# Swapping the first two gate products of an attention-plus-gMLP kernel on one Trainium2 core

## The chip, the cores and the metric

One Trainium2 chip, one core. The metric is the device time of one execution in microseconds (us), the median of several. "Span" is the time from the first to the last instruction of the one execution that a profile shows; it is some 1.7 to 1.8 us shorter than that execution's device time. Ratios are computed as the mean time of one kernel's runs over that of the other's of the same rounds, so they are not quite the ratio of the medians that are quoted beside them.

## The reference, cut to what matters

```python
xn = _layernorm(x)                        # 2048 tokens x 512
return x + A(xn, wqkv, wo) + B(xn, w_in, w_sp, b_sp, w_out)
# A: attention with 32 heads of 16, window of 8 keys two tokens apart
# B: z = gelu(xn @ w_in); z1 = first half (688); z2 = layernorm(second half)
#    g = w_sp @ z2 + b_sp; (z1 * g) @ w_out
```

Everything that follows happens in the first 27 of 201 us, where the normalised tokens are turned (transposed) so that TensorE can multiply them, and the first products for B (called z2 in the kernel) and A (q and k) are made.

## The kernel before

The 16 tiles of 128 tokens stand in four blocks: tile `4*tb + j` belongs to block `j`. The tokens `z2.0` and `z1.3` of the order string mean `z2_mm(2, 0)` and `z2_mm(1, 3)`, so the first tile of block 2 and the last of block 1; `zg` is the GELU that empties the product, `q2.2` a k product of block 2, `qc` the cast that empties it.

```python
ps_mm = ctx.enter_context(tc.tile_pool(name="ps_mm", bufs=3, space=PSUM))   # three PSUM buffers rotate
...
def tr_dma(i):                            # turn one tile by a DMA, issued from SyncE
    SP.dma_start_transpose(xnT[:, :, i * P:(i + 1) * P], xall[:, j, tb, :])

def zmm(i, wz):                           # 8 matmuls of 344 columns, L257
    pz = ps_mm.tile([P, 2, TBS], F32, name="pz", tag="mm")
    for hh in range(2):
        for kc in range(C):
            PE.matmul(pz[:, hh, 0:FHALF], xnT[:, kc, i * P:(i + 1) * P], wz[...], ...)

def z2_gelu(j, tb):                       # L275, empties pz
    A.activation(z2[:, i, :]..., tiles.pop(("z", j, tb))..., ACT.Gelu_apprx_tanh, accum_out=...)
...
    load_x(SP, 3, 0, 4)                   # x of block 3: four plain loads
    ...
    for i in i2:                          # block 2: normalise, then turn
        ln_apply(i)
        tr_dma(i)
    ...
    qk_part(pqs[0], 1, 3, 2, 4)           # last q/k product of block 1
    ln_root(blk_cols(3))                  # ScalarE: root of the variances of block 3
    qk_copy(pqs[0], 1, 3, 2, 4)           # ScalarE: cast that empties pqs[0]
    for i in i3:
        ln_apply(i)
        tr_dma(i)
    ...                                   # and then the steps of ORDER, one after the other
```

In these traces each engine's instructions stand in the order in which the program names them, so a product that waits holds up those named after it: in the kernel before z2.0 waited 0.60 us for its tile, and z1.3, whose tile had long landed, came behind it. The waits are on semaphores, which the trace records.

## Time and profile before

| | kernel before |
|---|---|
| time, median of the first three runs | 202.72 us (202.51 to 202.82) |
| time, median of all six runs of the comparison | 202.45 us (202.07 to 202.82) |
| span of the profiled execution | 200.8 us |
| TensorE (PE) busy | 196.3 us, 98% |
| VectorE (DVE) busy | 184.8 us, 92% |
| ScalarE (ACT) busy | 104.1 us, 52% |

TensorE works nearly without a break, so a change can win time in two ways: take work from TensorE, or fill one of its gaps. Its list of waits, its timeline and the chain tell which gaps there are; those lines stand in the prediction below. A busy share of 98% alone would not tell, because it doesn't say where the other 2% lie.

### The profile page before, as it was taken

The page shows a single profiled execution, that of the slowest core. Times are in us where ns is not written, and L with a number is a line of the kernel's source. Part 1 is how long each engine was busy: PE and PEld are TensorE (multiplying, and loading weights), DVE is VectorE, ACT ScalarE, POOL GpSimd, SP SyncE. Part 2 cuts the span into 40 slices and gives each one's busy share as a digit, 9 for nine tenths or more (in the row PEclk, how much of TensorE's full clock was granted, in tenths as well). Part 3 has the DMA queues.
Part 4 walks back from the last instruction along what each step waited for, and adds up shares of the span by engine and source line. Part 5 has one row for each costly group of instructions (what it writes and reads, how often), then busy time and mean ns, then how long its engine had stood idle before and what let it go on. Part 6 is the DMA issues. An engine that isn't in the chain of part 4 may idle for free.

```text
span 200.8 us, 4095 instructions
## 1 busy us (share of the span) xinstructions
PE 196.3 (98%) x1691; PEld 124.4 (62%) x1691; DVE 184.8 (92%) x249; ACT 104.1 (52%) x176; POOL 18.5 (9%) x14
## 2 busy tenths in 40 slices
PE   7999899999999999999999999999999999999994
PEld 2969655665566666666656666666544646664562
DVE  5789899999989999999979999999999999999624
ACT  3586887899899996363431523808502230331400
POOL 3000000899500000000000000000000000000000
PEclk9999999999999999999999999999999999999999
DMA  5876789930000085534376999199920278219863
GB/s 159 266 243 164 103 90 272 218 83 3 0 0 3 0 157 94 168 80 104 41 171 153 244 222 189 33 229 168 233 57 0 74 186 196 72 32 124 216 209 105
DMA packets 66562, 25.91 MB, mean 129 GB/s; under 512 B 56496, under 2 KB 66288, under 8 KB 66288
## 3 DMA queue, kind: packets, MB, share of 16 engines
q1 hardware_dynamic: 65824, 25.18, 57.4%
q10 hardware_dynamic: 720, 0.48, 0.8%
q8 instruction: 13, 0.21, 0.5%
q14 instruction: 5, 0.04, 0.1%
HBM read 10.13 MB, written 2.10 MB: 61 GB/s over the span
## 4 chain that ended last, share of the span: by engine, by line
PE 91%; DVE 3%; DMA 2%; ACT 2%; issue 0%
PE pg L464 37%; PE pz L257 19%; PE pq L315 7%; PE pv L425 7%; PE po L547 7%; PE po L517 6%; PE pwm L586 2%; PE pa L547 2%; DMA xnT<-r_x 2%; DVE stats L211 1%; PE pq L321 1%; PE pl L375 1%; ACT r_qk L331 1%; PE po L526 1%; PE pb L517 1%; DVE r_x L225 0%
## 5 line engine op out<-in xcount | busy, mean ns | idle before, releaser
L464 PE MATMUL pg<-z,r_qk 128*128 128x344 bf16 x448 | 66.8, 309 | 0.0
L464 PEld LDWEIGHTS <-r_qk 128*128 128x128 bf16 x448 | 43.8, 98 | 22.0 <-issue 0.4
L257 PE MATMUL pz<-w_z,xnT 128*128 128x344 bf16 x256 | 39.3, 309 | 0.6 <-DMA xnT<-r_x 0.6
L439 DVE TENSOR_TENSOR r_pr<-r_x,r_w 128x2048 bf16<-128x2048 bf16 x32 | 38.4, 1219 | 1.3 <-PE pl L375 1.0
L443 DVE TENSOR_TENSOR r_pr<-r_pr 128x2048 bf16<-128x2048 bf16 x28 | 33.9, 1218 | 0.4
L257 PEld LDWEIGHTS <-xnT 128*128 128x128 bf16 x256 | 24.9, 98 | 14.0 <-DMA xnT<-r_x 0.9
L470 ACT ACTIVATE gs<-pg,b_col 128x688 bf16<-128x688 f32 x16 | 13.2, 834 | 35.4 <-PE pg L464 26.4
L355 DVE TENSOR_TENSOR r_pr<-r_qk 128x2048 bf16<-128x2048 bf16 x24 | 27.8, 1219 | 0.7 <-ACT r_qk L331 0.5
L315 PE MATMUL pq<-xnT,r_w 128*128 128x512 bf16 (+1 forms) x136 | 24.7, 335 | 0.0
L315 PEld LDWEIGHTS <-r_w 128*128 128x128 bf16 x144 | 15.8, 114 | 7.6 <-issue 0.4
L684 POOL CAST b_col<-b 128x16 f32<-128x16 bf16 x1 | 16.5, 16457 | 33.4 <-DMA b<-in_B_b_sp_dram 33.4
L530 ACT CAST r_qk<-po 128x512 bf16<-128x512 f32 x10 | 5.5, 588 | 22.7 <-PE po L547 22.7
L331 ACT CAST r_qk<-pq 128x1024 bf16<-128x1024 f32 (+1 forms) x16 | 15.4, 983 | 2.7 <-PE pq L315 2.6
L306 ACT ACTIVATE r_uz<-pz 128x688 bf16<-128x688 f32 x16 | 11.7, 741 | 6.6 <-PE pz L257 6.5
L517 PE MATMUL po<-r_lg,r_pr 32*128 32x512 bf16 x192 | 14.5, 375 | 0.0
L425 PE MATMUL pv<-xnT,r_w 128*32 128x512 bf16 x256 | 14.2, 379 | 0.0
L547 PEld LDWEIGHTS <-r_uz 128*128 128x128 bf16 x85 | 8.0, 97 | 9.5 <-issue 1.1
L364 DVE TENSOR_TENSOR r_pr<-r_pr 128x4096 bf16<-128x4096 bf16 x6 | 13.7, 2286 | 0.0
L547 PE MATMUL po<-r_w,r_uz 128*128 128x512 bf16 x60 | 13.6, 380 | 0.0
L281 ACT ACTIVATE junk<-z 128x688 bf16<-128x688 bf16 x16 | 12.4, 774 | 0.1
L275 ACT ACTIVATE z<-pz 128x688 bf16<-128x688 f32 x16 | 11.8, 740 | 1.2 <-PE pz L257 1.2
L425 PEld LDWEIGHTS <-r_w 128*32 128x32 bf16 x256 | 9.5, 138 | 4.3
(85 smaller groups left out, 196.1 us busy)
## 6 DMA issues: line engine op xcount, KB each, us to landing
r_lg<-in_A_wo_dram SPq DMA_DIRECT2D x8, 256.0 KB, 4.0
r_x<-in_A_x_dram SPq DMA_DIRECT2D x12, 128.0 KB, 3.3
out_dram<-r_qk SPq DMA_DIRECT2D x12, 128.0 KB, 2.9
r_w<-in_A_wqkv_dram SPq DMA_DIRECT2D x8, 128.0 KB, 3.3
r_qk<-in_A_x_dram SPq DMA_DIRECT2D x8, 128.0 KB, 2.5
w_z<-in_B_w_in_dram SPq DMA_DIRECT2D x4, 172.0 KB, 4.3
w_z<-in_B_w_in_dram SPq DMA_DIRECT2D x1, 688.0 KB, 5.5
r_w<-in_B_w_out_dram SPq DMA_DIRECT2D x1, 640.0 KB, 6.2
```

Of the source, the lines that this page charges most:

```text
L257: PE.matmul(pz[:, hh, 0:FHALF], xnT[:, kc, i * P:(i + 1) * P], wz[:, kc, hh * FHALF:(hh + 1) * FHALF], start=(kc == 0), stop=(kc == C - 1))
L315: PE.matmul(pq[:, cc, p0 * P:(p0 + b1 - b0) * P], wqk[:, sd, kc, c0 + cc:D:C], xv[:, kc, b0:b1, j, :], start=(kc == 0), stop=(kc == C - 1))
L331: cast = A.copy(dst, pq[:, :, p0 * P:(p0 + b1 - b0) * P].rearrange("p c (b t) -> p c b t", b=b1 - b0))
L355: prod = V.tensor_tensor(pr[g % 3][:, c].rearrange("p w b t -> p b w t"), q3.unsqueeze(2).broadcast_to([P, TB, 4, P]), k4, ALU.mult)
L364: V.tensor_tensor(pr[g % 3][:, 0:2], pr[g % 3][:, 0:2], pr[g % 3][:, 2:4], ALU.add)
L425: PE.matmul(pv[32 * tb:32 * tb + 32, dd, :], wv[:, kc, 2 * d2 + dd, :], xnT[:, kc, tb * TBS:(tb + 1) * TBS], start=(kc == 0), stop=(kc == ...
L439: V.tensor_tensor(pw_t[n], vp[:, :, off:off + P], a_sb[:, slot_w(w), ts].unsqueeze(1).broadcast_to([P, DH, P]), ALU.mult)
L443: V.tensor_tensor(pw_t[n] if dst is None else dst, pw_t[n], pw_t[m], ALU.add)
L464: PE.matmul(pg[:, hh, 0:FHALF], wsp[n][:, k, :], z2[:, k, hh * FHALF:(hh + 1) * FHALF], start=(k == 0), stop=(k == NT - 1))
L517: PE.matmul(pc, op[32 * tb:32 * tb + 32, d, o * P:(o + 1) * P], wo_r[32 * tb:32 * tb + 32, d, cs], start=(d == 8), stop=False, tile_positi ...
L547: mm = PE.matmul(pc, uT[:, o % 2, m, tb * P:(tb + 1) * P], wout[:, m, cs], start=False, stop=(m == MCH - 3))
L684: G.tensor_copy(b_col[:], b16[:])
```

## The change

Its intent: TensorE waits for the tile of z2.0 to be turned, while the tile of z1.3 is there already. So z1.3 goes first, and the GELUs that empty the two products change places as well.

```diff
 ORDER = """
-z2.0 z1.3 p1.1 z2.2 zg2.0 p0.1 zg1.3 q2.2 zg2.2 p0.3 zs2.2 q2.3 p1.2 ...
+z1.3 z2.0 p1.1 z2.2 zg1.3 p0.1 zg2.0 q2.2 zg2.2 p0.3 zs2.2 q2.3 p1.2 ...
```

More of the change, by code (lines that the diff above doesn't have):

```diff
@@ L41 @@
 ORDER = """
-z2.0 z1.3 p1.1 z2.2 zg2.0 p0.1 zg1.3 q2.2 zg2.2 p0.3 zs2.2 q2.3 p1.2 qc2.2 p1.3 q2.1 qc2.3 p1.0 z1.0 p0.2
+z1.3 z2.0 p1.1 z2.2 zg1.3 p0.1 zg2.0 q2.2 zg2.2 p0.3 zs2.2 q2.3 p1.2 qc2.2 p1.3 q2.1 qc2.3 p1.0 z1.0 p0.2
 qc2.1 w3 z2.1 p0.0 zg1.0 zs1.0 q2.0 p2.2 zg2.1 a1 z2.3 qc2.0 w2 z1.2 zg2.3 p2.3 halo zs2.0 z3.0 p2.0 zg1.2
```

## The prediction

> **What bounds the kernel now.** I read the page first: the busy table, then the chain that ended last. After that came the waits of the matmul engine, its timeline, and the timelines of the other engines around the one place where it waits. The page's chain:
>
> ```profile
> PE 91%; DVE 3%; DMA 2%; ACT 2%; issue 0%
> ```
>
> Nine tenths of the chain is TensorE work. The list of TensorE's waits over the whole span shows how little is left to win by filling gaps (columns: engine, what it was about to do, for whom it waited, us in total, times, longest):
>
> ```profile
> PE pwm L586 <- DVE warm L189: 1.1, 1, 1.1
> PE pz L257 <- DMA xnT<-r_x: 0.6, 1, 0.6
> ```
>
> The first is the start of the program. The second is the only later gap, and it is where the change acts. TensorE's timeline (start, length, engine, line, operation, shapes, count, idle time before it):
>
> ```profile
> 18.00 3.66 PE L315 MATMUL pq<-xnT,r_w 128*128 128x256 bf16 x32
> 22.26 3.67 PE L257 MATMUL pz<-w_z,xnT 128*128 128x344 bf16 x24 [0.60 <-DMA xnT<-r_x]
> 25.77 5.34 PE L315 MATMUL pq<-xnT,r_w 128*128 128x512 bf16 x24
> ```
>
> The 32 matmuls of 256 columns end the q/k work of block 1. The 24 of 344 columns are the first three z products (8 each), in the order z2.0, z1.3, z2.2. Then come three q products of block 2. The wait stands before z2.0. The chain of that stretch says what it was:
>
> ```profile
> 17.84 0.58 DVE r_x L225 x2
> 18.42 3.79 DMA xnT<-r_x
> 22.22 0.05 issue
> 22.26 3.67 PE pz L257 x24
> ```
>
> The transposing transfer of the first tile of block 2 was issued at 18.42 and landed at 22.22. The last tile of block 1, which z1.3 reads, was transposed one round earlier: by the semaphore records of the trace it landed at 17.53, and the q/k products that started at 18.00 already read it.
>
> ScalarE matters too, since it empties the PSUM buffers. Its timeline in the same place:
>
> ```profile
> 22.57 0.30 ACT L221 ACTIVATE rstd<-mv,eps_t 128x4 f32<-128x4 f32 x1 [0.65 <-DVE mv L218]
> 22.77 0.57 ACT L331 CAST r_qk<-pq 128x512 bf16<-128x512 f32 x1
> 23.36 1.28 ACT L275 ACT_TABLE_LOAD   x1
> 24.65 0.74 ACT L275 ACTIVATE z<-pz 128x688 bf16<-128x688 f32 x1
> 25.29 0.20 ACT L275 ACTIVATION_READ_ACCUMULATOR z<-pz 128x1 f32 x1
> ```
>
> ScalarE waits for VectorE's statistics (mv), takes the root, casts, loads a table and only then runs the first GELU, whose accumulator read ends at 25.49. Nothing in that row waits for the first z product.
>
> **What the Trainium skill says.** "DMA: Bandwidth & Descriptors", in its account of where the fixed time of a transfer goes, puts the fixed part near 2 us and says that most of it is the receipt of the last write. The trace agrees in kind: the transpose's issue takes 1.20 us, and 2.6 us pass from the end of the issue to the landing (22.22 - 19.62), which no order on TensorE can shorten. "ScalarE: Activation LUTs", What ACT_TABLE_LOAD costs, gives some 1283 ns for the load; here it took 1.28 us. "PSUM — Partial Sum Buffer", on engine and sequencer instructions, says that matmuls start and complete in program order: so a product whose data are long there stands behind one whose data are not, which is the gap above. "Perfetto Trace Analysis", Optimizing Tensor Performance, asks that matmul groups rotate through PSUM banks so that emptying one overlaps the next; here three buffers rotate, and the fourth group must wait for the first GELU.
>
> **The change part by part.** It adds and removes no instruction. On TensorE two groups of eight matmuls change places, on ScalarE the two GELUs that empty them (zg1.3 before zg2.0). VectorE, the transfers and their order stay.
>
> *Step 1, the wait goes.* z1.3 now comes first. Its tile is there (17.53), the last part of its weights landed at 15.67, and its PSUM buffer was released by a cast at 21.01. The last 256-column matmul starts at 21.39; those follow each other 0.11 us apart, so z1.3 can start at about 21.50 in place of 22.26: 0.76 us earlier (the 0.60 of the view leaves out the overlap of pipelined matmuls).
>
> *Step 2, z2.0 second.* Eight matmuls of 344 columns take 1.17 us start to start (24 took 25.77 - 22.26 = 3.51). z2.0 starts at 21.50 + 1.17 = 22.67; its tile landed at 22.22 and its buffer came free at 21.93. No wait, 0.45 in hand.
>
> *Step 3, z2.2 third.* At 23.84; its tile landed at 23.61, its buffer came free at 23.35. No wait, but only 0.23 in hand.
>
> *Step 4, the fourth group, q2.2.* TensorE gets there at 25.00. The last tile of block 2 landed at 24.88, just in time. But the buffer is that of the first z product, and by the semaphore record the first GELU frees it at 25.50. ScalarE's row is not moved by the change: VectorE's statistics, root, cast and table load set 24.65, and z1.3 is done well before (its last record ends near 22.83). So q2.2 starts at 25.50 + 0.04 (the lag that the trace shows between landing and start) = 25.54. Before, it started at 25.77. Of 0.76 us there remain 25.77 - 25.54 = **0.23 us**; the other half microsecond becomes a wait for ScalarE. That wait should read 25.54 - 25.16 = 0.38, if the last z matmul starts at 24.85 and lasts its 0.31.
>
> *Step 5, does the 0.23 reach the end?* For each later group of matmuls I compared the start with the latest of the semaphore values that it waits for. From q2.2 on the slacks are over 0.7 us everywhere except twice: the second buffer of the head products at 143.41, freed by ScalarE at 143.09 (0.32), and a transposed tile at 184.50, landed at 184.16 (0.34). Both exceed 0.23. The buffer release follows TensorE's own z product and moves with it anyway. VectorE, busy from 102 us on almost without a gap, hands over its last result 1.08 us before TensorE takes it at 189.45, and its one long wait (0.95 at 102.36) was for TensorE. The tail, four additions and stores, hangs on the last matmuls. So all of the 0.23 should arrive: 202.72 - 0.23 = 202.49, call it **202.5**.
>
> **The rivals.** *The whole gap is won*: 202.72 - 0.76 = 201.96. It would need the fourth group not to depend on the first GELU, or that GELU to run earlier. Against it: the table load starts right at the end of a cast that itself follows a root waiting for VectorE, none of which waits for z. *Nothing is won*: the lead is lost at one of the tight hand-offs or in a tail set by VectorE or a transfer, giving 202.7. For it speaks that two slacks of 0.3 are near and the early transfers vary (3.1 to 4.2 us from issue to landing); against it that the lead is smaller than both. *A new wait for a transfer replaces the old one*: z2.2 or q2.2, which now come up to 0.76 earlier, find their tile missing, having 0.23 and 0.12 in hand. But the 0.38 wait for the GELU follows, so a late tile only fills time that is lost anyway; the landings would have to slip by about half a microsecond before they cost anything, and even one late by 1 us costs less than 1 us in 202. *Slower through ScalarE*: if the swap delayed the first GELU, q2.2 would come later than 25.77; z1.3 being ready nearly 2 us before its GELU speaks against it.
>
> **Range and chances.** All of these lie between 201.9 and 203; a move of 2% would be 4 us, more than the whole gap. The three runs before spread over 0.31 us (202.51 to 202.82), as much as the effect itself. I give the 0.23 theory about three quarters, nothing gained a fifth, the whole gap one in twenty. The range that should hold 8 times in 10 is 202.2 to 202.8. Chances: faster by over 2% 0.01, within 2% 0.98, slower 0.01.
>
> **What the profile after would show.** Step 1 is right if the line of the wait for the transfer is gone from TensorE's waits and the first 344-column matmul starts near 21.5. Step 4 is right if in its place stands a wait of pq L315 for ACT z L275 near 0.38, the first GELU still starts near 24.65, and the three q products start near 25.54; the chain of the stretch should then run back through the GELU, the table load, the root and VectorE's statistics. Step 5 is right if the products after the last head products (189.51 in the chain before) come about 0.23 earlier, with no new wait between. Wrong would be: q2.2 at 25.0 (whole gap), a first GELU later than 24.65, z2.2 held by a transfer for more than half a microsecond, or a lead at 26 us that is gone at 189.

## The result, and the profile after

| | before | after |
|---|---|---|
| median of six runs | 202.45 us (202.07 to 202.82) | 202.15 us (201.97 to 202.35) |
| span of the profiled execution | 200.8 us | 200.5 us |

The ratio is 0.9986 with a 95% interval of 0.9971 to 1.0002: 0.30 us between the medians, not quite clear of the noise. The time lies 0.05 us below the range that was predicted.

The waits of TensorE in the changed kernel (for whom, us in total, times, longest):

```profile
PE pwm L586 <- DVE warm L189: 1.1, 1, 1.1
PE po L547 <- issue: 0.5, 3, 0.2
PE pq L315 <- ACT z L275: 0.3, 1, 0.3
```

The wait for the transfer (DMA xnT) is gone, and a wait for a GELU (ACT z, line 275) stands in its place. The three small gaps called "issue" are not waits: 1687 matmuls are recorded in place of 1691, and where a record is missing the view shows a gap. The timeline of TensorE:

```profile
18.01 3.66 PE L315 MATMUL pq<-xnT,r_w 128*128 128x256 bf16 x32
21.50 3.66 PE L257 MATMUL pz<-w_z,xnT 128*128 128x344 bf16 x24
25.46 5.34 PE L315 MATMUL pq<-xnT,r_w 128*128 128x512 bf16 x24 [0.29 <-ACT z L275]
```

The z products start at 21.50 in place of 22.26, but the q products at 25.46 in place of 25.77. Of 0.76 us, 0.31 are left after 4 us. ScalarE's timeline, in the same place as the one shown of before:

```profile
22.49 0.30 ACT L221 ACTIVATE rstd<-mv,eps_t 128x4 f32<-128x4 f32 x1 [0.56 <-DVE mv L218]
22.70 0.57 ACT L331 CAST r_qk<-pq 128x512 bf16<-128x512 f32 x1
23.28 1.28 ACT L275 ACT_TABLE_LOAD   x1
24.57 0.74 ACT L275 ACTIVATE z<-pz 128x688 bf16<-128x688 f32 x1
25.21 0.20 ACT L275 ACTIVATION_READ_ACCUMULATOR z<-pz 128x1 f32 x1
```

Root, cast, table load and GELU follow each other as before, only 0.08 us earlier. The chain of this stretch now runs through them:

```profile
22.49 0.30 ACT rstd L221
22.79 0.47 ACT r_qk L331
23.26 0.02 issue
23.28 1.28 ACT L275
24.56 0.01 issue
24.57 0.84 ACT z L275 x2
25.42 0.04 issue
25.46 4.69 PE pq L315 x21
```

In the chain of before a transfer of 3.79 us led to the first z product; now VectorE's statistics, the root, the cast, the table load and the first GELU lead to the q product. At the other end, the last pieces of the chain of before:

```profile
195.82 1.77 PE pa L547 x10
197.59 0.02 issue
197.62 0.77 DVE r_pr L535 x2
```

and of after:

```profile
195.51 1.77 PE pa L547 x10
197.28 0.02 issue
197.30 0.77 DVE r_pr L535 x2
```

They come 0.31 and 0.32 us earlier. What was left at 26 us arrived whole.

### The profile page after: what moved, and what is told of

Its sections match the earlier page's. It is cut to its first block, busy times and chain, and to the rows that moved or that the text cites. A ratio compares the mean times of both kernels' runs of the same rounds, so it can differ in the third digit from the quotient of the medians.

```text
span 200.5 us, 4090 instructions
## 1 busy us (share of the span) xinstructions
PE 195.8 (98%) x1687; PEld 124.4 (62%) x1691; DVE 184.8 (92%) x249; ACT 104.1 (52%) x176; POOL 18.5 (9%) x14
## 4 chain that ended last, share of the span: by engine, by line
PE 90%; DVE 5%; ACT 3%; issue 1%
PE pg L464 37%; PE pz L257 17%; PE pq L315 7%; PE pv L425 7%; PE po L517 6%; PE po L547 6%; DVE stats L211 3%; PE pwm L586 2%; PE pa L547 2%; PE pq L321 1%; ACT r_qk L331 1%; PE pl L375 1%; DVE r_x L225 1%; DVE mv L218 1%; PE po L526 1%; PE pb L517 1%
## 5 line engine op out<-in xcount | busy, mean ns | idle before, releaser
L547 PE MATMUL po<-r_w,r_uz 128*128 128x512 bf16 x56 | 12.7, 379 | 0.5 <-issue 0.5
```

Source lines behind the costliest of these rows:

```text
L547: mm = PE.matmul(pc, uT[:, o % 2, m, tb * P:(tb + 1) * P], wout[:, m, cs], start=False, stop=(m == MCH - 3))
```

## The experiments

Two things had to be settled: what cuts the lead at q2.2, and how much of the 0.3 us is the change and how much is drift. My theory: the PSUM buffer that the first GELU frees. Rivals: the last transposed tile of block 2; a lead lost later; no gain at all.

Executions differ in when they reach block 1: the last q/k group of block 1, 32 matmuls of 256 columns, started between 17.57 and 18.24 us in all profiles but that of e12, although the kernels don't differ up to there. So I measure within each trace from that start, called A from here on (not the A of the reference). The values come from the timelines and the semaphore records. "GELU" is the end of the first GELU's accumulator read, "landed" the landing of the tile that z2.0 reads, "took" its time from issue to landing, "end" the end of VectorE's last instruction, a closing semaphore step 2.35 to 2.38 us after its last addition.

| profile | A | first z | GELU | landed (took) | q2.2 | end |
|---|---|---|---|---|---|---|
| before | 18.00 | +4.26 | +7.49 | +4.21 (3.79) | +7.77 | +182.75 |
| after | 18.01 | +3.49 | +7.40 | +4.11 (3.69) | +7.45 | +182.44 |
| e1_after_again | 17.94 | +3.49 | +7.27 | +3.97 (3.55) | +7.32 | +182.29 |
| e2_pe_only | 17.76 | +3.49 | +7.27 | +4.01 (3.60) | +7.32 | +182.28 |
| e3_aux_buffer | 18.11 | +3.49 | +7.27 | +4.13 (3.38) | +7.29 | +182.28 |
| e4_cast_first | 17.57 | +3.49 | +6.80 | +3.89 (3.48) | +7.26 | +182.23 |
| e5_double_cast | 18.24 | +3.49 | +7.88 | +3.90 (3.48) | +7.93 | +182.90 |
| e6_double_cast_before | 18.23 | +3.71 | +7.88 | +3.66 (3.26) | +7.93 | +182.91 |
| e7_cast_first_before | 17.76 | +4.08 | +6.83 | +4.03 (3.61) | +7.59 | +182.56 |
| e8_four_ready | 18.05 | +3.49 | +6.80 | +3.98 (3.56) | +8.16 | +181.96 |
| e9_before_again | 17.89 | +3.94 | +7.27 | +3.90 (3.48) | +7.45 | +182.42 |
| e10_after_third | 17.86 | +3.52 | +7.33 | +4.10 (3.73) | +7.38 | +182.35 |
| e11_four_again | 17.99 | +3.49 | +6.79 | +3.98 (3.56) | +8.16 | +181.97 |
| e12_loads_early | 19.28 | +3.52 | +6.76 | +2.27 (3.40) | +7.02 | +181.99 |

In e8 and e11 one more product of 1.17 us stands before q2.2. In all others the distance from q2.2 to the end is between 174.96 and 175.00 us: **whatever moves q2.2 moves the end by as much**. No later hand-off takes part of the lead, in any of these traces. (TensorE's list of waits leaves out gaps under 0.15 us, so small waits are read from the semaphore records.)

The runs came in three calls, each on another chip, so times are compared within a call. The first call ran e1 to e4 with eleven runs of the kernel before (median 202.33 us, 201.76 to 202.94).

### e1_after_again

No edit: the changed kernel again.

> The changed kernel again, with more rounds. Theory (the lead of TensorE is cut by the PSUM buffer that the first GELU frees): three products start near 25.46 to 25.54 us, 0.25 to 0.35 us ahead of the kernel before, and the time is 0.2 to 0.35 us shorter (ratio 0.9983 to 0.9990). Rival (the difference seen was drift between runs): ratio within 0.0005 of 1. The kernel before should again spread over more than 0.3 us.

Median 202.00 us (201.96 to 202.25), ratio 0.9985 (0.9968 to 1.0002). q2.2 started at 25.26 us, 0.05 after the first GELU's end; from A it came at +7.32. The theory holds in the trace. The gain is again 0.3 us and again its interval just includes none. The kernel before spread over 1.18 us.

### e2_pe_only

```diff
-z1.3 z2.0 p1.1 z2.2 zg1.3 p0.1 zg2.0 q2.2 zg2.2
+z1.3 z2.0 p1.1 z2.2 zg2.0 p0.1 zg1.3 q2.2 zg2.2
```

> Only the matmuls change places, the two GELUs keep their old order, so the buffer that q2.2 waits for is freed by the second GELU in place of the first. Theory (PSUM buffer): q2.2 starts near 26.2 us, later than in the kernel before (25.77), and the time is about 0.4 us LONGER than before. Rival (q2.2 is held by the landing of its last tile, or by nothing of ScalarE): q2.2 stays near 25.46 and the time about 0.3 us shorter, as with the whole change.

Median 202.01 us, ratio 0.9984 (0.9967 to 1.0000): as the whole change. I had expected it 0.4 us slower, and was wrong about the pool. In the built program of e2, q2.2 is placed in the buffer at PSUM bank 4, that of z2.0, whereas in the changed kernel it is in the one at bank 0, that of z1.3. So here the pool gave the next product the buffer that is released first in the order of the program, not the oldest. q2.2 still started 0.04 us after the first GELU's end (25.08, 25.04). So this run doesn't tell the theory from a rival; it shows that the second half of the change, the swap of the GELUs, isn't needed.

### e3_aux_buffer

```diff
 def qk_mm(j, m):
+    if (j, m) == (2, 2):                     # q2.2: two idle one-bank buffers, no GELU to wait for
+        for cc in range(2):
+            pa = ps_aux.tile([P, TBS], F32, name="pa4", tag="aux")
+            ...the same 4 matmuls per half, written to pa...
+        return
     tiles["q", j, m] = qk_tile()
```

(and its cast in two halves)

> The changed kernel, but q2.2 is written into two idle one-bank buffers, so that it waits for no GELU. Theory (PSUM buffer): the wait for ACT z is gone, q2.2 starts near 25.00 (its last tile lands near 24.88), 0.77 us ahead of the kernel before, and the time is 0.6 to 0.8 us shorter than before. Rival (transfer): q2.2 stays near 25.46, 0.3 us shorter. Rival (a later hand-off eats a longer lead): q2.2 at 25.00, but the time no more than 0.4 us shorter, with a new wait late in TensorE's list.

Median 201.77 us, ratio 0.9970 (0.9953 to 0.9987). The wait for ACT z is gone from TensorE's list, and q2.2 waits for no semaphore of ScalarE any more, so the buffer was the reason for that wait:

```profile
PE pwm L603 <- DVE warm L189: 1.1, 1, 1.1
PE pq L321 <- DMA r_w<-in_A_wqkv_dram: 0.3, 1, 0.3
```

But q2.2 started at +7.29 from A, not at the 7.0 I expected. The reason is in the semaphore records: the third product waited for its tile (landed 24.06, product 24.11) and q2.2 for the last tile of block 2 (landed 25.35, product 25.40). So the rival "transfer" is right too, as the next limit; in e1 that last tile had landed 0.41 us before q2.2 (24.85, 25.26). The median of e3 is 0.23 us below that of e1 in the same rounds, while q2.2 comes only 0.03 earlier in the trace. One trace of each can't settle how much e3 gains on the mean, because the landings vary, and the execution profiled here was the slowest of the six (202.15 us). By the ratio the gain is 0.6 us, the low end of what was expected.

### e4_cast_first

```diff
     qk_part(pqs[0], 1, 3, 2, 4)
-    ln_root(blk_cols(3))
     qk_copy(pqs[0], 1, 3, 2, 4)
+    ln_root(blk_cols(3))
```

> The changed kernel, with the cast of the last block 1 product placed before the root on ScalarE: it fills the time in which ScalarE waits for VectorE, so table load and first GELU come about 0.5 us earlier. Theory: first GELU near 24.1, its buffer free near 24.9, q2.2 near 25.00, time 0.6 to 0.8 us shorter than before. Rival (transfer): GELU earlier but q2.2 near 25.46 and 0.3 us shorter. If the cast delays the root, VectorE's block 3 norm and the transposes come later: no gain.

Median 201.73 us, ratio 0.9970 (0.9953 to 0.9988). The cast fills the time in which ScalarE waited for VectorE, and the GELU's end comes at +6.80 in place of +7.27. The root was not late: it follows VectorE's statistics as before. TensorE no longer waits for the GELU, but q2.2 moves only from +7.32 to +7.26: again the third product waits for its tile (landed 23.41, product 23.45), and the last tile of block 2 landed at 24.70, 0.13 before q2.2 at 24.83. Same reading as e3, by another way; by the ratio the gain is 0.6 us here too. In both traces these tiles landed later from A than in the others except e12: the third product's at +5.95 and +5.84 in place of +5.49 to +5.65, the last at +7.24 and +7.12 in place of +6.76 to +6.94. At the usual landings neither would have held up a q2.2 at +7.0, so how often the tiles are the next limit isn't shown.

The second call ran e5 to e8 with eleven other runs of the kernel before (median 202.10 us, 201.77 to 202.45).

### e5_double_cast

```diff
     qk_copy(pqs[0], 1, 3, 2, 4)
+    qk_copy(pqs[0], 1, 3, 2, 4)
```

> The changed kernel with the short cast before the table load done twice, so that the first GELU comes about 0.5 us later. Measured from the start of the last 256-column matmuls of block 1, three products (q2.2) started 7.77 us later in the kernel before and 7.45 and 7.32 in the changed one. Theory (the first GELU gates q2.2 with no slack): q2.2 at 7.8 to 7.9, the whole gain gone, time within 0.15 us of the kernel before. Rival (a transfer gates q2.2): q2.2 stays near 7.4 and the time 0.3 us shorter than before.

The second cast doesn't overlap the first (1.18 us for the two, 0.57 for one), so it costs 0.61. The GELU's end goes from +7.27 to +7.88 and q2.2 from +7.32 to +7.93: each by 0.61, with the same 0.05 between them. In the changed kernel, then, q2.2 hangs on the first GELU without slack. ScalarE's row of e5:

```profile
22.79 1.18 ACT L331 CAST r_qk<-pq 128x512 bf16<-128x512 f32 x2
23.99 1.28 ACT L275 ACT_TABLE_LOAD   x1
25.29 0.74 ACT L275 ACTIVATE z<-pz 128x688 bf16<-128x688 f32 x1
```

The median is 202.77 us, ratio 1.0036 (1.0022 to 1.0049), which is slower than I expected.

### e6_double_cast_before

The same edit in the kernel before.

> The same doubled cast in the kernel before, whose buffer release had 0.23 us to spare: theory: q2.2 at about 8.0 us from the start of the 256-column matmuls (7.77 without), time about 0.25 us longer than before; the wait for the transposed tile stays at 0.6 and a second wait, for ACT z, of about 0.2 appears. Rival (ScalarE is not near the path): q2.2 stays at 7.77 and the time the same.

Median 202.81 us, ratio 1.0031 (1.0019 to 1.0043). The waits of TensorE for the GELU in e5 and in e6:

```profile
PE pq L315 <- ACT z L275: 0.8, 1, 0.8
```

```profile
PE pq L315 <- ACT z L275: 0.6, 1, 0.6
```

q2.2 stands at +7.93 in both, and the times are level (202.77 and 202.81). So **with the GELU late, the order of the two products is worth nothing**: the time that the swap saves ahead of the GELU is waited away behind it. The wait for the tile, which I expected to stay at 0.6, was small here, because in this execution the tile landed at +3.66. Both e5 and e6 lost some 0.2 to 0.4 us more than their q2.2 explains (0.7 us by the medians, and 0.32 from the mean of +7.61 in the two traces of before, or 0.48 from +7.45 in e9). Their profiles reached A at 18.24 and 18.23, later than all others up to there (e7 and e8 at 17.76 and 18.05); the edit changes no instruction before A, and I leave it open.

### e7_cast_first_before

The edit of e4 in the kernel before.

> The kernel before with the cast placed before the root, as in e4_cast_first. Theory: TensorE still waits for the transposed tile before z2.0 and q2.2 stays where the matmuls put it, 7.7 to 7.8 us from the start of the 256-column matmuls: no gain from this alone, time within 0.15 us of the kernel before, so that what e4_cast_first gained beyond the swap is an interplay of the two. Rival (the cast order is worth something by itself): 0.3 us or more shorter.

Median 202.21 us, ratio 1.0011 (0.9998 to 1.0024): no gain. The GELU's end is early (+6.83), but q2.2 comes where the matmuls put it: 3.51 after the first z product at +4.08. Which of two waits counts depends on the other: with the old order the tile counts, with the new order the GELU.

### e8_four_ready

The edit of e4, and z1.0, another product of block 1, second:

```diff
-z1.3 z2.0 p1.1 z2.2 zg1.3 p0.1 zg2.0 q2.2 zg2.2 p0.3 zs2.2 ... p1.0 z1.0 p0.2
-qc2.1 w3 z2.1 p0.0 zg1.0 zs1.0 ...
+z1.3 z1.0 p1.1 z2.0 zg1.3 z2.2 p0.1 zg1.0 q2.2 zg2.0 p0.3 zg2.2 zs2.2 ... p1.0 p0.2
+qc2.1 w3 z2.1 p0.0 zs1.0 ...
```

> The cast first, and two products of block 1 (z1.3, z1.0) before the two of block 2, so that the tiles of block 2 have 1.17 us more time to land. In e3_aux_buffer and e4_cast_first the third product waited for its tile (0.05 us after landing) or q2.2 for the next one. Theory: no wait is left on TensorE after the start; four z products start back to back and q2.2 starts 3.50 + 4 x 1.17 = 8.17 us from the start of the 256-column matmuls (one product of work more stands before it, so 8.94 would be level with the kernel before); time 0.6 to 0.8 us shorter than before. Rival (a later hand-off eats the lead): no wait here, but a new one later and a gain below 0.4 us.

Median 201.76 us, ratio 0.9979 (0.9968 to 0.9991): faster than the kernel before beyond the noise, though by 0.4 us and not the 0.6 to 0.8 expected. TensorE's timeline:

```profile
18.05 3.66 PE L315 MATMUL pq<-xnT,r_w 128*128 128x256 bf16 x32
21.54 4.83 PE L257 MATMUL pz<-w_z,xnT 128*128 128x344 bf16 x32
26.21 5.34 PE L315 MATMUL pq<-xnT,r_w 128*128 128x512 bf16 x24
```

There is no wait between these groups: 32 z matmuls stand back to back, and q2.2 starts at +8.16 (8.17 expected). The end comes 0.79 us earlier from A than in the first trace of before, but 0.46 earlier than in the second (e9): the size that I expected was measured against an execution with an unusually long wait.

The third call ran e9 to e12 with eleven more runs of the kernel before (median 202.11 us, 201.82 to 202.69).

### e9_before_again

No edit: the kernel before, for a second trace.

> The kernel before itself, for a second trace of it and for the size of the noise. The transposing transfer that z2.0 waits for took 3.79 us from issue to landing in the profile of before, but 3.26 to 3.69 in nine other profiles. Theory (that profile had the longest of its kind): this profile shows it at 3.3 to 3.7 and TensorE's wait for it at 0.1 to 0.5 us in place of 0.6; ratio 1 within 0.001. Rival (the wait of 0.6 is typical): 0.55 to 0.65 again.

Median 202.19 us, ratio 1.0001 (0.9986 to 1.0017). TensorE's timeline:

```profile
17.89 3.66 PE L315 MATMUL pq<-xnT,r_w 128*128 128x256 bf16 x32
21.84 3.67 PE L257 MATMUL pz<-w_z,xnT 128*128 128x344 bf16 x24 [0.29 <-ACT r_qk L331]
25.34 1.89 PE L315 MATMUL pq<-xnT,r_w 128*128 128x512 bf16 x8
```

The wait is 0.29 here, not 0.60. The view names a cast, but the first product doesn't wait for the one that ended at 21.82; by the semaphore values its own wait ended with the tile at 21.79. The transfer took 3.48 us. So the gap that the change fills is not one number: 0.77 us of start-to-start time in the first trace of before (4.26 - 3.49), 0.45 in the second (3.94 - 3.49).

### e10_after_third

No edit: the changed kernel a third time.

> The changed kernel a third time, beside the kernel before of the same rounds. Theory: q2.2 follows the first GELU by 0.04 us, 7.3 to 7.45 us after the start of the 256-column matmuls; ratio between 0.998 and 0.9995, smaller in effect than the 0.33 us of the first pair of traces if those had an unusually long transfer. Rival (no real gain): ratio 1 within 0.0005.

Median 201.93 us (201.83 to 202.57), ratio 0.9996 (0.9979 to 1.0013). q2.2 again follows the GELU by 0.04 (+7.38). By the ratio the gain in these rounds is 0.08 us (0.18 between the medians), in the earlier ones 0.28 and 0.30. Alone this run would speak for the rival, no real gain within 0.0005. The mean of the three ratios is 0.9989, or 0.22 us of 202.2. Taking the three as independent, their half widths combine to 0.0010: an interval of about 0.9979 to 0.9999. So a gain is likely, and its size is open between almost nothing and 0.4 us.

### e11_four_again

No edit: e8 again.

> The best version so far once more: no wait on TensorE after the start, 0.3 to 0.7 us shorter than before (ratio 0.9965 to 0.9985) and shorter than the changed kernel of the same rounds by 0.2 to 0.4 us. If it is level with the changed kernel, its gain in e8 was drift.

Median 201.72 us (201.66 to 201.80), ratio 0.9980 (0.9966 to 0.9993). All six runs are faster than each of the six of e10. q2.2 and the end repeat to 0.01 us. This version beats both kernels, by 0.4 us the one before and by 0.2 the changed one (201.93 in the same rounds). That it also beats e4, which lacks the extra product of block 1, is not shown: e4's ratio of 0.9970 (0.9953 to 0.9988) overlaps with those of e8 and e11.

### e12_loads_early

```diff
+    load_x(SP, 3, 0, 4)                     # at the start, after the loads of w_z2
 ...
     tr_dma(i1[3])
-    load_x(SP, 3, 0, 4)
```

(the order of the kernel before)

> The order of the kernel before, but the four loads of block 3 of x, which are issued just ahead of the transposes of block 2, are issued before the transposes of block 1. In ten profiles the first transpose after these loads took 3.3 to 3.8 us to land, those further back 2.4 to 2.5. Theory (the loads hold the first transpose up): the one that z2.0 waits for takes about 2.5 us, the wait before z2.0 is gone without any swap, q2.2 is gated by the first GELU at 7.3 to 7.45 us from the start of the 256-column matmuls; but the first transpose of block 1 now stands behind the loads and takes over 3.2 us. Rival (the first transpose of a row is slow by itself): still 3.3 us or more and the wait stays. On time: faster by 0.2 to 0.4 us if block 1 has room for its later transposes (0.47 us in the profile of before), else even or slower.

Median 202.52 us, ratio 1.0016 (1.0000 to 1.0032). The wait before z2.0 is gone, but a larger one appears earlier; TensorE's list has

```profile
PE pq L316 <- DMA xnT<-r_x: 1.1, 1, 1.1
```

SyncE's queue was busy with the moved loads until 15.24 us, so the first transpose of block 1 was issued at 15.36 in place of 13.67. The last tile of block 1 landed at 19.23, and A came at 19.28. And my theory of why that one transfer is slow fell: with no loads just ahead of it, the first transpose of block 2 still took 3.40 us, the two behind it 2.72 and 2.50. In all fourteen profiles it took 3.26 to 3.79. (The profile of e12 is of the slowest of its six executions, 203.01 us.)

Why the transpose is slow is open, but the records of single DMA packets show a suspect that none of the expectations names. In each of the fourteen traces one packet of 8192 bytes, of a queue that the view calls "instruction", starts between 19.34 and 20.73 us, while this transpose is under way. In e12 it ran from 19.39 to 20.04; the rate in slices of 0.075 us from 19.00 on then falls to some 10 GB/s for about 0.7 us, with no loads of x about (`prof e12_loads_early --dma --window 19:22`):

```profile
GB/s 0 0 0 0 41 256 218 208 212 195 215 188 133 72 28 10 10 7 10 7 7 7 10 7 18 27 85 177 208 212 215 191 225 201 168 35 4 0 0 0
q14 instruction: 1, 0.01, 1.4%
```

In the first trace of before, 28 packets of the transposes that started near 21.0 took 0.39 to 0.64 us, where the median in a quiet transpose is 0.018, and all of them, with the last load of x, ended by 21.61. The next packet of this kind (16384 bytes, starting between 26.53 and 28.71) falls into a transpose of block 3 that took 3.93 to 5.03 us; the third and fourth of block 2, with no such packet, took 2.47 to 2.52. It is a coincidence in every trace and not a cause that was shown: no run moved these packets, and block 1's first transpose took up to 3.29 us in traces without one.

## Why the prediction was right or wrong

**Wrong: the level and the width of the range.** The measured median, 202.15 us, lies 0.05 below the predicted 202.2 to 202.8. The step that failed is the last sum of step 5, 202.72 - 0.23 = 202.49, in its first term: the kernel before measured 202.45 over six runs, 0.27 less than the 202.72 of the three, while the second term came out at 0.30. The range was built on the same runs: "The three runs before spread over 0.31 us (202.51 to 202.82), as much as the effect itself". Three more runs of the same kernel beside the changed one gave 202.07, 202.39 and 202.07, and 39 runs in the later rounds had medians of 202.10 to 202.33 and ranged from 201.76 to 202.94. Three runs told neither the level nor the spread; why these three came out high isn't known. The difference was forecast far better than the absolute time: 0.23 us predicted, 0.30 between the medians.

**Steps 1 to 3, right.** z1.3 started at 21.50 as predicted, z2.0 at 22.67 and z2.2 at 23.84, with 0.55 and 0.23 us in hand (0.45 and 0.23 predicted). The wait for the transfer was gone.

**Step 4, right in mechanism, off by 0.08 us in size.** The wait for ACT z came in place of the other, as long as 0.29 in place of 0.38, and q2.2 started at 25.46 in place of 25.54. ScalarE's row came 0.08 earlier because VectorE's last statistics did: they started at 21.55 in place of 21.62, just after the last load of x landed (21.52 and 21.60). So the GELU's time was one draw as well: in the other traces with the loads in their old place these statistics started 3.44 to 3.50 us after A, in place of 3.62 and 3.54. e5 shows that the GELU is the gate, and e6 that a later GELU gates the old order too; e7 and e8 show when it isn't.

**The size of step 1 was one draw.** 0.76 us was right for the trace that it was read from, but e9 had 0.45 for the same kernel. Between the two traces of before and the three of after, q2.2 came at a mean of 7.61 and 7.38 from A: 0.23 us, the predicted figure, partly by luck. The times can't confirm it more closely: each of the three ratios has an interval that includes 1, and their mean is only just clear of it.

**Step 5, right.** From q2.2 to the end, 174.98 us before and 174.99 after. The two tight hand-offs held, at 143.09 with 0.31 in hand and at 184.18 with 0.53. The second was tighter than the prediction read it: its 0.34 goes by the start of the matmul, but the weight load that reads the tile stood at 184.29, 0.13 after the landing. It cost nothing, since the transpose moved with the lead (issued 0.32 us earlier, landed 0.51 earlier).

**The rivals.** "The whole gap is won" fell. "A new wait for a transfer" was judged rightly for the change as it is. Its margins of 0.23 and 0.12 us were small indeed: where the GELU's wait was taken away (e3, e4), the tiles of block 2 came 0.2 to 0.5 us later and took its place. The "3.1 to 4.2 us" that the prediction gives for the early transfers is of a view that could match only 4 of 10 landings; by the semaphore records those ten took 2.44 to 4.23.

## What to carry to other kernels

A wait that is removed is worth only the distance to the next one, so list, for the next few groups of work, every signal that each waits for and when it arrives; here three limits lay within half a microsecond, and only a version that moved all three (earlier GELU, two products with data long there, later use of the late tiles) ran without a gap, and even its time is not shown to differ from that of the version with the earlier GELU alone (e4). Before claiming tenths of a microsecond, take a second trace and more than three runs of the unchanged kernel. Compare traces from a common event inside them rather than from their start.

## What the Trainium skill lacked or had wrong

- "ScalarE: Activation LUTs", What ACT_TABLE_LOAD costs, adds a drain of about 1380 ns to the load of 1283 ns. In the traces of before and after the load took 1.28 us, began 0.02 us after the end of the cast before it, and the GELU began 0.01 us after it (and so at all seven loads after the start): no such drain shows, and with it step 4 would have been wrong by more than the whole gap of 0.76 us.
- "DMA: Bandwidth & Descriptors" gives its fixed cost of about 2 us, and where that goes, for DMAs issued from GpSimd (Anatomy of one DMA); I found neither for a transpose issued from SyncE. Here a quiet one (block 2's fourth, in the trace of before) took 2.47 us: 1.22 of issue, 0.77 from the first packet to the last, 0.50 from there to the landing.
- No page that I read says that a transpose's time depends on what else is under way. The first of block 2's row took 3.26 to 3.79 us in fourteen profiles, its third and fourth 2.47 to 2.52; that packets of the "instruction" queues are the reason is not shown.
- No page that I read says how much a single wait differs between executions of the same kernel: 0.60 us in one profile of the kernel before, 0.29 in another.
